# Attention output laid out by token block, and one ScalarE copy per PSUM bank for a batch of two steps

## The chip, the cores and the metric

The kernel runs on one core of one Trainium2 chip. The metric is the device time of one execution in microseconds; the median of 3 runs before the change is 198.72 us (198.62 to 199.81). The engines are named as in the profile: PE is TensorE's matmul side and PEld its weight load, DVE is VectorE, ACT is ScalarE, POOL is GpSimd, SP is SyncE, which starts most of the DMAs.

## What is computed

A linear attention with decay runs over 4 batches, 8 heads and 768 tokens with heads of 64, and its result goes through a two-layer network with a tanh gelu:

```python
for b in range(nb):                       # blocks of 64 tokens
    intra = einsum('bhic,bhjc->bhij', qb, kb) * Dmask
    intra = einsum('bhij,bhjd->bhid', intra, vb)
    inter = einsum('bhid,bhde->bhie', qb * lam_pow, kv_state)
    out[:, :, sl] = intra + inter
    kv_state = lam_block * kv_state + einsum('bhsd,bhse->bhde', kb * rev_pow, vb)
x = out.transpose(0, 2, 1, 3).reshape(3072, 512)
h = x @ w_in                              # 512 x 2048
g = 0.5 * h * (1 + tanh(c * (h + 0.044715 * h**3)))
return g @ w_out                          # 2048 x 512
```

## The kernel before

**Steps.** The attention is worked in 24 steps. A step is one block of 256 tokens of one batch and one half of the heads (4 of 8, as two pairs): step s is block s // 2 and half s % 2. Twelve blocks in all, three to a batch. Inside a step the kernel works with two chunks of 128 tokens. For each step there are: the casts of q (VectorE), k (ScalarE) and v (GpSimd) to fp16; the transposes of q and k, by TensorE for the steps up to 7 and by DMA from step 8 on (`FIRST_DMA_T`); the scores (L350); their mask on VectorE (`causal`, L360); the products with v, and the products with the carried state u, both into the same PSUM bank, one bank for each chunk; the products of k and v for the new state; the state's update on VectorE (L534) and its fp16 copy u on GpSimd (L542 or L549). Last `x_out` copies the two banks into the fp16 tile xT, which the network reads. Steps either go one at a time (`R`, which calls `scores` and `products`) or, from step 12 on, in `burst`, which takes two steps together: the banks O0 and O1 then hold both steps' 256 columns side by side. The bursts of two steps evacuate 13/14, 16/17, 18/19, 20/21 and 22/23; step 15 goes alone in `R` and step 12 alone in a burst.

**NARROW.** For the steps 13, 14, 16, 17, 20 and 21 the product with u is made by four matmuls of 64 rows and not two of 128, and in bank 1 the two heads of a pair stand with their partition halves exchanged. For these `x_out` copies bank 1 by two copies of 64 partitions (L509), each into the other half; the full copies are L513.

**Groups.** Blocks are gathered in seven groups, [0,1], [2], [3], [4,5], [6,7], [8,9] and [10,11]. Once a group's attention is finished, `queue_group` puts its network work, as small pieces, at the end of a list; `fill(n)` issues the next n pieces. First-layer pieces (L597, L874) make 512 columns in one bank, which a gelu on ScalarE (L601) copies out. Groups 1 to 6 make the second layer with sums of blocks (L646) and seven products (L676) in place of eight; groups 5 and 6 do so for the first layer too (`seven`, L775, with sums of x on VectorE at L754). Where a group has two blocks and the plain first layer, one matmul reads both blocks: two runs of 256 columns of xT.

**Order.** The order of the instructions on each engine is written out by hand (`pin` keeps it); an engine works its own list in order and waits at semaphores that the framework places from the tiles read and written. PSUM has eight banks, taken in turn by all tiles. The part that the change touches stands thus for steps 13 and 14: `burst((15, 16), (13, 14))` issues scores of 15 and 16, products of 13 and 14 (L446), the state products (L461), a wait, the u products (L474), the masks on VectorE, then the copies of both steps on ScalarE; `fill` follows with first-layer pieces, whose gelus queue behind those copies.

Of the kernel before, what the change touches and what calls it, by code (L numbers as in the profile page):

```python
# [9 lines left out]
FP16 = mybir.dt.float16  # L10
# [5 lines left out]
def kernel(  # L16
# [10 lines left out]
    nc = tc.nc  # L27
    pin = tc.keep_in_program_order
    P = 128
    B, H, S, D = q.shape  # L30
    SB = 256
# [19 lines left out]
    xtp = ctx.enter_context(tc.tile_pool(name="xtp", bufs=3))  # L51
# [287 lines left out]
    def half64(i):  # L339
        return slice(64 * i, 64 * i + 64)  # L340
# [21 lines left out]
                mask[:].unsqueeze(1).to_broadcast([P, 2, 2 * P]), ALU.mult))  # L362
        PTs[n] = t

    def products(n, s, banks=None, evacuate=True):


        OK, opened = banks or ([ps_M.tile([P, 512], FP32, tag="M", name=f"OK{c}")
                                for c in range(2)], set())

        def start(c, hl):
            if (c, hl) in opened:
                return False
            opened.add((c, hl))
            return True

        if n is not None:
            _, tk, tv = a16[n]
            last = (n // 2) % NSB == NSB - 1
            for jk in range(2):  # L380
                for hp in range(2):
                    for c, hl in TILES:
                        if c == 1 and last:
                            continue
                        pin(nc.tensor.matmul(
                            OK[c][half64(hl), 256 + hp * D : 256 + hp * D + D],
                            tk[half64(c), jk, 2 * hp + hl, :], tv[half64(c), jk, 2 * hp + hl, :],
                            start=start(c, hl), stop=(jk == 1), skip_group_check=True))
            Kps[n] = [t[:, 256:384] for t in OK]
        if s is None:  # L390
            return OK, opened
        sbg, half = divmod(s, 2)
        o = qkT.pop(s)
        PT = PTs.pop(s)
        _, _, tv = a16.pop(s)
        for hp in range(2):
            for jk in range(2):
                for c, hl in TILES:
                    pin(nc.tensor.matmul(  # L399
                        OK[c][half64(hl), hp * P : hp * P + P], tv[half64(c), jk, 2 * hp + hl, :],  # L400
                        PT[half64(c), hl, hp, jk, :], start=start(c, hl), stop=False,
                        skip_group_check=True))
        for c in range(2):
            if c == 0 and sbg % NSB == 0:
                continue
            u = us.pop((s, 0) if c else (s - 2, 1))
            for hp in range(2):
                pin(nc.tensor.matmul(OK[c][:, hp * P : hp * P + P], u[:, hp].rearrange("p l d -> p (l d)"),  # L408
                                     o[:, 0, :, hp, half64(c)], start=False, stop=True,
                                     skip_group_check=True))  # L410
        if evacuate:
            x_out(s, OK)
        return OK, opened

    def behind(ins):
# [7 lines left out]
    def burst(ns, ss, *mix, ahead=None):  # L423


        narrow = bool(NARROW & set(ss))
        for i, n in enumerate(ns):
            scores(n)
            if ahead and i == 0:
                ahead()  # L430
        O = [ps_M.tile([P, 2, 2, P], FP32, tag="M", name=f"O{c}") for c in range(2)]
        seen = set()

        def start(kind, c, hl):
            new = (kind, c, hl) not in seen
            seen.add((kind, c, hl))
            return new

        qTs = [qkT.pop(s) for s in ss]
        for i, s in enumerate(ss):  # L440
            PT, tv = PTs.pop(s), a16.pop(s)[2]
            for hp in range(2):
                for jk in range(2):
                    for c, hl in TILES:
                        to = hl ^ narrow * c
                        mm = nc.tensor.matmul(  # L446
                            O[c][half64(to), i, hp, :], tv[half64(c), jk, 2 * hp + hl, :],
                            PT[half64(c), hl, hp, jk, :], start=start("O", c, to), stop=False,
                            skip_group_check=True)
                        pin(mm)  # L450
        if ns:
            K = [ps_M.tile([P, 2, P], FP32, tag="M", name=f"K{c}") for c in range(2)]
        for i, n in enumerate(ns):
            _, tk, tv = a16[n]
            last = (n // 2) % NSB == NSB - 1
            for jk in range(2):
                for hp in range(2):
                    for c, hl in TILES:
                        if c == 1 and last:
                            continue  # L460
                        pin(nc.tensor.matmul(  # L461
                            K[c][half64(hl), i, hp * D : hp * D + D],
                            tk[half64(c), jk, 2 * hp + hl, :], tv[half64(c), jk, 2 * hp + hl, :],
                            start=start("K", c, hl), stop=(jk == 1), skip_group_check=True))
            Kps[n] = [t[:, i] for t in K]
        if narrow:
            behind(mm)
        for i, s in enumerate(ss) if narrow else ():
            u = [us.pop(key, None) for key in ((s - 2, 1), (s, 0))]
            for hp in range(2):  # L470
                for c, hl in TILES:
                    if u[c] is None:
                        continue
                    pin(nc.tensor.matmul(  # L474
                        O[c][half64(hl ^ c), i, hp, :], u[c][half64(hl), hp, :],
                        qTs[i][half64(hl), 0, :, hp, half64(c)], start=False, stop=True,
                        skip_group_check=True))
        for i, s in enumerate(ss) if not narrow else ():
            for c in range(2):
                if c == 0 and (s // 2) % NSB == 0:  # L480
                    continue
                u = us.pop((s, 0) if c else (s - 2, 1))
                for hp in range(2):
                    pin(nc.tensor.matmul(O[c][:, i, hp, :], u[:, hp].rearrange("p l d -> p (l d)"),
                                         qTs[i][:, 0, :, hp, half64(c)], start=False, stop=True,
                                         skip_group_check=True))
        for n in ns:
            causal(n)
        for i, s in enumerate(ss):
            x_out(s, [t[:, i].rearrange("p h t -> p (h t)") for t in O], swapped=narrow)  # L490
        sbg = ss[-1] // 2
        g, i = group_of[sbg]
        if ss[-1] % 2 == 1 and i == len(groups[g]) - 1:
            queue_group(g, *mix)
        for n in ns:
            update(n, 0)

    def x_out(s, OK, second=None, swapped=False):
        sbg, half = divmod(s, 2)
        g, i = group_of[sbg]  # L500
        if g not in xT:
            xT[g] = xtp.tile([P, 2, len(groups[g]), 2, SB], FP16, tag="xT", name=f"xT_{g}")
        dst = xT[g][:, half, i]
        for c in range(2):
            d = dst[:, :, c * P : (c + 1) * P].rearrange("p hp (t j) -> p hp j t", j=2)
            o = OK[c][:, 0:256].rearrange("p (hp j t) -> p hp j t", hp=2, j=2)
            if c == 1 and swapped:
                for hl in range(2):
                    pin(nc.scalar.activation(out=d[half64(hl)], in_=o[half64(1 - hl)], func=AF.Copy))  # L509
            elif c == 1 and second is not None:  # L510
                pin(second.tensor_copy(out=d, in_=o))
            else:
                pin(nc.scalar.activation(out=d, in_=o, func=AF.Copy))  # L513
# [66 lines left out]
    def queue_group(g, lead=0, per_set=0):  # L580
# [4 lines left out]

        def x(c):

            return xT[g][:, c // 2, :, c % 2, :]

        def by_block(t):  # L590
            return t.rearrange("p (b t) -> p b t", t=SB)
# [151 lines left out]
        def x_block(t, cs):  # L743
            if t in X_SUMS:
                return xsum[0][:, (t - 1) // 2, (t - 1) % 2, cs, :]
            C, T = t
            return xT[g][:, C, T, cs, :]

        def sum_x(m):
            if not xsum:  # L750
# [194 lines left out]

    def R(n, s, ahead=None, keep=False):

        if n is not None:
            scores(n)
        if ahead:  # L950
            ahead()
        products(n, s)
        if n is not None:
            causal(n)
        if s is not None and s % 2 == 1:
            g, i = group_of[s // 2]
            if i == len(groups[g]) - 1 and g > 0:
                queue_group(g)
        if n is not None and not keep:
            update(n, 0)  # L960
# [236 lines left out]
```

## Time and profile before

| | |
|---|---|
| median of 3 runs | 198.72 us (198.62 to 199.81) |
| the profiled execution | 198.66 us, of which the span is 196.9 us |
| PE busy | 191.0 us |
| ACT busy | 125.0 us |
| DVE busy | 145.9 us |
| POOL busy | 68.9 us |
| copies of 128x256 out of OK banks (one step) | 26, mean 452 ns, 9.9 us |
| copies of 128x256 out of O banks (bursts) | 16, mean 459 ns, 6.6 us |
| copies of 64x256 out of O banks (bursts, NARROW) | 12, mean 454 ns, 5.5 us |

The span goes from the first to the last instruction of the profiled execution, and its own time is some 1.8 us longer. A line of the profile's groups names the source line, the engine, the operation, the tile written and the tiles read, the count, the busy time and the mean duration; a line of the order of time gives the start, the duration, and in brackets how long the engine stood idle before it and what ended that. A line of the list of waits gives who waited for whom, the total in us, the number of times and the longest. The profile's slices are fortieths of the span, in tenths of busy time.

### The profile page before, as it was taken

The page shows a single profiled execution, that of the slowest core. Times are in us where ns is not written, and L with a number is a line of the kernel's source. Part 1 is how long each engine was busy: PE and PEld are TensorE (multiplying, and loading weights), DVE is VectorE, ACT ScalarE, POOL GpSimd, SP SyncE. Part 2 cuts the span into 40 slices and gives each one's busy share as a digit, 9 for nine tenths or more (in the row PEclk, how much of TensorE's full clock was granted, in tenths as well). Part 3 has the DMA queues.
Part 4 walks back from the last instruction along what each step waited for, and adds up shares of the span by engine and source line. Part 5 has one row for each costly group of instructions (what it writes and reads, how often), then busy time and mean ns, then how long its engine had stood idle before and what let it go on. Part 6 is the DMA issues. An engine that isn't in the chain of part 4 may idle for free.

```text
span 196.9 us, 5962 instructions
## 1 busy us (share of the span) xinstructions
PE 191.0 (97%) x2451; PEld 139.4 (71%) x2453; DVE 145.9 (74%) x291; ACT 125.0 (63%) x255; POOL 68.9 (35%) x85
## 2 busy tenths in 40 slices
PE   8979999999999999999999999999999999999993
PEld 2556544446888888654678854578888888888882
DVE  4797722889999889849989925999657987487620
ACT  3673878357874685676855379844867866679221
POOL 6594213456554841068623415056002030002000
PEclk9999999999999999999999999999999999999999
DMA  5999999999999999999996998710211300020205
GB/s 169 290 323 385 386 387 388 296 295 288 244 217 222 257 343 223 214 270 264 252 279 148 269 314 115 163 33 0 53 59 51 109 4 2 0 110 28 82 16 199
DMA packets 62811, 38.13 MB, mean 194 GB/s; under 512 B 18624, under 2 KB 55744, under 8 KB 62784
## 3 DMA queue, kind: packets, MB, share of 16 engines
q1 hardware_dynamic: 62240, 37.50, 76.6%
q8 instruction: 19, 0.31, 0.7%
q10 hardware_dynamic: 544, 0.26, 0.5%
q14 instruction: 8, 0.07, 0.1%
HBM read 27.26 MB, written 6.29 MB: 170 GB/s over the span
## 4 chain that ended last, share of the span: by engine, by line
PE 87%; SPq 4%; DMA 4%; ACT 3%; issue 1%
PE Hps L597 23%; PE MX L676 18%; PE MY L676 9%; PE HX L775 7%; PE O2ps L612 7%; PE MW L676 4%; DMA wi<-in_moe_w_in_dram 4%; SPq L70 4%; PE HY L775 4%; PE S L350 3%; PE Hps L874 3%; PE HW L775 2%; PE OK L408 2%; PE O L446 1%; PE OK L399 1%; PE Tps L321 1%
## 5 line engine op out<-in xcount | busy, mean ns | idle before, releaser
L597 PE MATMUL Hps<-xT,w_in 128*128 128x512 f16 (+1 forms) x288 | 50.5, 332 | 0.0
L597 PEld LDWEIGHTS <-w_in 128*128 128x128 f16 x288 | 27.8, 98 | 19.3
L601 ACT ACTIVATE gT<-Hps 128x512 f16<-128x512 f32 x56 | 32.4, 598 | 9.8 <-PE Hps L597 9.2
L360 DVE TENSOR_TENSOR PT<-S,mask 128x512 f16<-128x512 f32 x48 | 30.3, 682 | 8.3 <-PE S L350 8.3
L676 PEld LDWEIGHTS <-gs 128*128 128x128 f16 x320 | 31.2, 98 | 3.6
L266 POOL TENSOR_TENSOR v<-v,dv 128x512 f16<-128x512 f32 x24 | 27.0, 1128 | 18.5 <-PE Hps L597 9.6
L549 POOL TENSOR_TENSOR u<-t,lumask 128x256 f16<-128x256 f32 x29 | 21.4, 748 | 29.8 <-DVE t L534 20.5
L676 PEld LDWEIGHTS <-gT 128*128 128x128 f16 x240 | 23.1, 98 | 3.7 <-ACT gT L601 0.6
L676 PE MATMUL MX<-w_sum,gs 128*128 128x256 f16 x160 | 21.4, 273 | 0.0
L646 DVE TENSOR_TENSOR gs<-gT 128x1024 f16<-128x1024 f16 (+1 forms) x24 | 17.8, 750 | 3.3 <-ACT gT L601 3.3
L282 DVE TENSOR_TENSOR qk<-q,dq 128x512 f16<-128x512 f32 x23 | 18.1, 792 | 1.5 <-DMA q<-in_q_dram 1.3
L295 ACT ACTIVATE qk<-k 128x512 f16<-128x512 f32 x23 | 14.4, 626 | 7.4 <-DMA k<-in_k_dram 6.9
L728 POOL TENSOR_TENSOR o<-u,q 128x512 f32<-128x512 f32 (+1 forms) x5 | 5.9, 1184 | 36.9 <-ACT u L693 36.9
L612 PE MATMUL O2ps<-w_out,gT 128*128 128x512 f16 x64 | 14.6, 379 | 0.0
L513 ACT ACTIVATE xT<-OK 128x256 f16<-128x256 f32 x26 | 9.9, 452 | 6.5 <-PE OK L408 6.1
L775 PEld LDWEIGHTS <-ws 128*128 128x128 f16 x128 | 12.4, 98 | 1.7 <-DVE xs L754 0.2
L693 ACT ACTIVATE u<-MX 128x256 f32<-128x256 f32 x18 | 6.9, 384 | 7.3 <-PE MX L676 7.3
L612 PEld LDWEIGHTS <-gT 128*128 128x128 f16 x64 | 6.1, 98 | 6.6
L676 PE MATMUL MY<-w_out,gs 128*128 128x256 f16 x80 | 10.7, 273 | 0.0
L350 PEld LDWEIGHTS <-qkT 64*64 64x64 f16 x384 | 6.0, 106 | 6.6 <-issue 3.6
L542 POOL TENSOR_TENSOR u<-t,lamu 128x128 f16<-128x128 f32 x11 | 6.1, 559 | 12.8 <-DVE t L534 7.2
L789 DVE COPY u<-HX 128x512 f32<-128x512 f32 x8 | 5.5, 688 | 6.8 <-ACT gT L793 4.3
(102 smaller groups left out, 326.5 us busy)
## 6 DMA issues: line engine op xcount, KB each, us to landing
q<-in_q_dram SPq DMA_DIRECT2D x24, 256.0 KB, 4.8
k<-in_k_dram SPq DMA_DIRECT2D x24, 256.0 KB, 5.0
v<-in_v_dram SPq DMA_DIRECT2D x23, 256.0 KB, 5.3
out_dram<-o SPq DMA_DIRECT2D x23, 256.0 KB, 4.1
wo<-in_moe_w_out_dram SPq DMA_DIRECT2D x4, 1024.0 KB, 9.5
wi<-in_moe_w_in_dram SPq DMA_DIRECT2D x4, 512.0 KB, 8.1
wi<-in_moe_w_in_dram SPq DMA_DIRECT2D x2, 1024.0 KB, 12.7
v<-in_v_dram ACTq DMA_DIRECT2D x1, 256.0 KB, 4.2
```

What stands on the lines that cost most here:

```text
L266: pin(nc.gpsimd.tensor_tensor(wide(tv[:]), ld32[s][2][:], decay(dv, s), ALU.mult))
L282: pin(q_eng.tensor_tensor(wide(tq), q32[:], decay(dq, s), ALU.mult))
L295: pin(nc.scalar.activation(out=wide(tk), in_=k32[:], func=AF.Copy))
L350: pin(nc.tensor.matmul(Sps[hl][half64(c), hp, jk, :], o[half64(hl), 1, jk, hp, half64(c)], o[half64(hl), 0, :, hp, half64(c)], start=True, ...
L360: pin(nc.vector.tensor_tensor(t[:, hl].rearrange("p b c d -> p b (c d)"), Sps[:].rearrange("p b c d -> p b (c d)"), mask[:].unsqueeze(1).t ...
L549: pin(nc.gpsimd.tensor_tensor(u[:], state[half][:].unsqueeze(2).to_broadcast([P, 2, 2, D]), lumask[:, 2 * half : 2 * half + 2, :].unsqueez ...
L597: pin(nc.tensor.matmul(by_block(Hps[:, i, :]), w_in16[:, c, f * P : (f + 1) * P], x(c), start=(c == 0), stop=(c == NC - 1)))
L601: pin(nc.scalar.activation(out=dst, in_=Hps[:], func=AF.Gelu_apprx_tanh))
L612: pin(nc.tensor.matmul(O2[tau][0][:], gT[:, f % HF, f // HF, tau * P : (tau + 1) * P], w_out16[:, f, :], start=(n == 0), stop=(n == NF - 1)))
L646: pin(nc.vector.tensor_tensor(g_rows(m, i), g_rows(a, i), g_rows(b, i), op))
L676: pin(nc.tensor.matmul(dst, lhsT, rhs, start=(opens and i == 0), stop=(closes and i == HF - 1), skip_group_check=True))
L775: pin(nc.tensor.matmul(dst[:, i, :], w_in_block(a, slice(c, c + 1), slice(f * P, f * P + P))[:, 0], x_block(b, slice(c, c + 1))[:, 0], sta ...
```

## The change

xT held, for each group, the axes half, block, pair, token; it now holds block, half, pair, token. Steps that follow one another (half 1 of one block and half 0 of the next among them) thus stand side by side. `x_out` takes a list of steps and one slice of each bank that covers all of them, and makes one copy for each bank (or, in bank 1 of NARROW steps, two of 64 partitions) for the whole list. `burst` calls it once. The readers of xT take the new axes. `products` and `R` also get a branch for steps in NARROW.

```diff
@@ products
-            x_out(s, OK)
+            x_out((s,), [t[:, 0:256] for t in OK], swapped=s in NARROW)
@@ burst
-        for i, s in enumerate(ss):
-            x_out(s, [t[:, i].rearrange("p h t -> p (h t)") for t in O], swapped=narrow)
+        x_out(ss, [t[:, 0 : len(ss)].rearrange("p i h t -> p (i h t)") for t in O], swapped=narrow)
@@ x_out
-    def x_out(s, OK, second=None, swapped=False):
-        sbg, half = divmod(s, 2)
+    def x_out(ss, O, second=None, swapped=False):
+
+        sbg, half = divmod(ss[0], 2)
         g, i = group_of[sbg]
         if g not in xT:
-            xT[g] = xtp.tile([P, 2, len(groups[g]), 2, SB], FP16, tag="xT", name=f"xT_{g}")
-        dst = xT[g][:, half, i]
+            xT[g] = xtp.tile([P, len(groups[g]), 2, 2, SB], FP16, tag="xT", name=f"xT_{g}")
+        r = 4 * i + 2 * half
+        dst = xT[g].rearrange("p b a h t -> p (b a h) t")[:, r : r + 2 * len(ss)]
         for c in range(2):
-            d = dst[:, :, c * P : (c + 1) * P].rearrange("p hp (t j) -> p hp j t", j=2)
-            o = OK[c][:, 0:256].rearrange("p (hp j t) -> p hp j t", hp=2, j=2)
+            d = dst[:, :, c * P : (c + 1) * P].rearrange("p r (t j) -> p r j t", j=2)
+            o = O[c].rearrange("p (r j t) -> p r j t", j=2, t=D)
@@ queue_group
-            return xT[g][:, c // 2, :, c % 2, :]
+            return xT[g][:, :, c // 2, c % 2, :]
...
-            return xT[g][:, C, T, cs, :]
+            return xT[g][:, T, C, cs, :]
@@ products, for s in NARROW (before: none)
+        if s in NARROW:
+            between()
+            behind(mm)
+            u = [us.pop(key, None) for key in ((s - 2, 1), (s, 0))]
+            for hp in range(2):
+                for c, hl in TILES:
...
@@ R
+        def first():
+            if n is not None:
+                scores(n)
+            if ahead:
+                ahead()
+
+        if s in NARROW:
+            products(n, s, between=first)
+        else:
+            first()
+            products(n, s)
```

More of the change, by code (lines that the diff above doesn't have):

```diff
@@ L363, in causal, with products @@
         PTs[n] = t
-    def products(n, s, banks=None, evacuate=True):
+    def products(n, s, banks=None, evacuate=True, between=None):
         OK, opened = banks or ([ps_M.tile([P, 512], FP32, tag="M", name=f"OK{c}")
@@ L398, in products @@
                 for c, hl in TILES:
+                    to = hl ^ (c if s in NARROW else 0)
+                    mm = nc.tensor.matmul(
+                        OK[c][half64(to), hp * P : hp * P + P], tv[half64(c), jk, 2 * hp + hl, :],
+                        PT[half64(c), hl, hp, jk, :], start=start(c, to), stop=False,
+                        skip_group_check=True)
+                    pin(mm)
+        if s in NARROW:
[4 more added lines that the diff above has]
+                for c, hl in TILES:
+                    if u[c] is None:
+                        continue
                     pin(nc.tensor.matmul(
-                        OK[c][half64(hl), hp * P : hp * P + P], tv[half64(c), jk, 2 * hp + hl, :],
-                        PT[half64(c), hl, hp, jk, :], start=start(c, hl), stop=False,
+                        OK[c][half64(hl ^ c), hp * P : hp * P + P], u[c][half64(hl), hp, :],
+                        o[half64(hl), 0, :, hp, half64(c)], start=False, stop=True,
                         skip_group_check=True))
-        for c in range(2):
+        for c in range(2) if s not in NARROW else ():
             if c == 0 and sbg % NSB == 0:
@@ L946, in R @@
     def R(n, s, ahead=None, keep=False):
[L948 to L952, printed above, removed]
+        def first():
[8 more added lines that the diff above has]
+            products(n, s)
         if n is not None:
```

## The prediction

> **What bounds the kernel now.** I read the page's busy shares and slices first, then the chain of waits, the list of who waited for whom, and last the order of time around each of the five places where a batch of two steps leaves its banks.
>
> ```profile
> span 196.9 us, 5962 instructions
> ...
> PE 191.0 (97%) x2451; PEld 139.4 (71%) x2453; DVE 145.9 (74%) x291; ACT 125.0 (63%) x255; POOL 68.9 (35%) x85
> ...
> PE   8979999999999999999999999999999999999993
> ...
> PEclk9999999999999999999999999999999999999999
> ```
>
> TensorE is busy in every slice but the first and the last, at its full clock. The 5.9 us in which it is not busy (196.9 - 191.0) lie almost wholly in two places: 20.00 - 17.55 = 2.45 us in the first 20 us, and 6.90 - 3.61 = 3.29 us after 190 us, in the final copy and store (both from the table of busy time by stretch). Neither holds a batch of two steps. So ScalarE's 63% says nothing by itself: the change pays only where TensorE waits for ScalarE.
>
> The chain of waits, asked for 94 to 101 us, seems to show a large prize. 26.0 + 12.9 = 38.9% of these 7 us lie on the copies to be merged:
>
> ```profile
> 94.92 0.35 PE O L474 x12
> 95.28 0.45 ACT xT L513
> ...
> 95.73 0.46 ACT xT L509
> ...
> 96.20 0.45 ACT xT L509
> ...
> 96.67 0.46 ACT xT L513
> ...
> 98.08 0.79 ACT gT L601 x2
> ...
> 99.05 0.61 ACT gT L601
> ...
> 99.71 1.16 PE MX L676 x9
> ```
>
> A chain only says what released what. It doesn't say that TensorE stood still meanwhile. The order of time on TensorE and the list of waits say what was really lost:
>
> ```profile
> 95.18 3.63 PE L597 MATMUL Hps<-xT,w_in 128*128 128x512 f16 x16
> 98.65 2.22 PE L676 MATMUL MX<-w_out,gT 128*128 128x256 f16 x16
> ```
>
> ```profile
> PEld L676 <- ACT gT L601: 0.4, 1, 0.4
> ```
>
> TensorE worked through 16 matmuls of the first layer from 95.18 us and began the second layer's first product at 98.65. Seven of that product's eight matmuls were issued; the eighth needs the gelu that ended at 99.66 and started at 99.712, while its predecessor had started at 99.303. A matmul of 256 columns takes 0.109 us from start to start here (0.87 us for eight in the whole chain), so **the loss is 99.712 - 99.303 - 0.109 = 0.30 us**. I took the start-to-start distance of all neighbouring TensorE matmuls in the same way: after 20 us this is the only gap above 0.2 us. The others are 0.10 to 0.16 us each, nearly all where matmuls of 64 and of 128 rows change over, and hang on no copy that the change touches.
>
> **What the Trainium skill says.** "ScalarE: Activation LUTs", section "What ACT_TABLE_LOAD costs", prices an ACTIVATE without pointer operands at 186 ns + 0.833 ns per column and says that back-to-back ones overlap by about 93 ns. The trace agrees for plain copies: 384 ns at 256 columns against 399, 598 ns at 512 against 612. The xT copies, with their interleaved fp16 output, show 455 ns at 256 columns, some 70 more. "PSUM — Partial Sum Buffer", section "PSUM bank collisions raise a hardware error", has two engines kept off one bank and quadrant even at different columns. The trace fits: in the batch of steps 13 and 14 the first copy, whose own columns were done with the O matmuls at about 94.7 us, started only at 95.27, after the last L474. It was waiting on the bank, so a copy of the whole bank has nothing more to wait for.
>
> **The change part by part.**
>
> *Layout of xT.* Step s writes 512 consecutive columns before and after. The sums on VectorE read 512 consecutive columns before and after. The first layer's two-block matmuls read two runs of 256 columns, now 1024 columns apart and not 512. Their present spacing is 6.91 us / 32 = 0.216 us, the same as the second layer's 7.77 / 36 = 0.216 with one unbroken run, so a break in the run costs nothing at today's distance. I take 0 for the wider distance; the other end stands with the rivals.
>
> *Fewer copies.* Five batches have two steps. The three in the NARROW set (13/14, 16/17, 20/21) go from 2 full and 4 half-partition copies to 1 and 2; the two others (18/19, 22/23) from 4 to 2. In all 26 copies become 13. One copy of 512 columns isn't in the trace. From below: 598 ns, the gelu of 512 columns out of a bank. From above: 455 + 256 x 0.833 = 668 ns, with the skill's slope, which the trace's own (598 - 384) / 256 = 0.836 repeats. I take 0.65. In the NARROW batches the copies stand end to end, 0.47 us from start to start (six from 95.27 to the next gelu at 98.08 = 2.81 us); three of 0.65 + 0.01 make 1.98 us, so 0.83 us is saved each. Range: 3 x 0.61 to 3 x 0.68, saving 0.77 to 0.98. In the unshifted batches the copies overlap, 0.29 to 0.33 us apart; the last batch's four end after 161.59 - 160.21 = 1.38 us, and two of 512 columns, about 0.50 apart, end after 0.50 + 0.65 = 1.15 us: 0.23 us saved. Sum: 3 x 0.83 + 2 x 0.23 = 3.0 us of ScalarE.
>
> *Where it lands on the path.* At 95.27 only. The last four gelus there start at 98.08, 98.58, 99.05 and 99.53, back to back behind the copies. With copies that end near 97.25, the third gelu is limited by its own matmuls: 12 of the 16 end at about 95.18 + 12 x 0.218 = 97.80, and in the steady stretch before, a gelu starts 0.2 us after its piece; so it runs from 98.0 to 98.6 us, 0.8 us before TensorE wants it at 99.41. **The whole 0.30 us goes**, and would go for any copy up to (2.81 - 0.30) / 3 = 0.83 us. What is late next there is nothing: the second product of that phase wants the fourth gelu only after 100.4 us.
>
> *The other four batches* give 0. At 118.28 and 155.61 ScalarE falls behind as much, but TensorE goes on with the first layer and with the second products, and no TensorE wait shows there; at 126.29 the sums start at 129.15, 1.2 us after the copies end. The last batch could lose. There the first sum wants step 22 from both banks, 160.98 before, about 161.36 after, or 160.21 + 2 x 0.668 = 161.55 without overlap. VectorE comes to that sum at 161.46 in any case, so the cost is 0 (taken) to 0.1 us, and the matmuls HY wait for this sum already (0.17 us on the weight loads).
>
> *The new branch for NARROW steps in the single-step products.* The steps that pass through it are 0 to 11 and 15, and none is in the set, so its extra wait and changed order are never emitted: 0.
>
> *Does the 0.30 us stay?* TensorE runs 0.3 us earlier from 99.7 on. What could be late by then is a transpose by DMA: those for step 21 land at 123.98 us against use at 125.15, and wait on TensorE itself for their buffer; step 19's land at 113.7 against 116.6. Covered, with over 1 us.
>
> Sum, against the profiled execution's own 198.66 us (span 196.87 and 1.8 around it): 198.66 - 0.30 = 198.36. That execution lies 0.06 below the median of the three runs shown, so 198.4 on their scale.
>
> **The rivals.**
> *No gain.* The freed ScalarE time is taken back, by a 512-column copy above 0.83 us or because the awaited gelu is then held by something that the chain hides. For it: only one place pays, and by 0.15% of the time. Against: the six gelus from 89.38 to 93.69 us, with no copies ahead of them, each found ScalarE idle for 0.27 to 0.40 us first. Time: 198.7, or 198.8 with the last batch's 0.1.
> *Slower, by the reads of xT.* Two-block matmuls of 512 columns are 160 in L597 and 16 in L874. If two runs 2048 bytes apart stream worse than runs 1024 bytes apart, each pays; TensorE has no slack, so all of it shows. Above 0.30 / 176 = 1.7 ns each the change is slower than before; at 10 ns it is 198.36 + 1.76 = 200.1. Against: today's break in the run costs nothing measurable, 0.216 us with it and without.
> *More than forecast.* Also the 0.17 us at HY and some of the mode changes vanish: 198.2. Against: the former hangs on VectorE's queue.
>
> **How the numbers follow.** Forecast 0.64 (198.2 to 198.6), no gain 0.25 (198.6 to 199.0), slower by the reads 0.06 (mostly 199 to 201), more than forecast 0.05. Two of the three runs shown are 0.1 us apart and the third is 1.1 higher, so I give 0.2 us for the median's own scatter: the range is 198.0 to 199.0, which leaves out the slower rival. About 1%, 2 us, is what a measurement of this kernel can tell from no change, and neither main case reaches it; slower by more needs over 13 ns per two-block matmul: 0.04. Faster by more has no cover in the profile, since TensorE's waits for ScalarE after 20 us don't add up to 1 us: 0.02.
>
> **What would show it.** 13 xT copies out of O banks with 512 columns at 0.60 to 0.67 us, and none in place of the 26; ScalarE busy about 122 to 124 us in place of 125.0, less than the copies' sum where overlaps vanish. In the stretch after steps 13/14 the gelus follow their matmuls, and the weight loads' wait of 0.4 us for gT is gone. First-layer matmuls of 512 columns still 379 ns and 0.216 us apart. The prediction is wrong if that wait stays, if the matmuls' spacing grows, or if a new wait of TensorE appears at the last batch, near 161.9 us, or at a burst.

## The result and the profile after

The changed kernel takes 198.44 us (median of 18 runs, 198.29 to 199.01) against 198.75 us before (18 runs beside them): ratio 0.9982, 95% interval 0.9974 to 0.9989. The forecast was 198.4 us, and that no more than one TensorE stall of 0.30 us would go. The profiled execution took 198.45 us with a span of 196.7 us, so 1.79 us lie outside the span, as before.

The edit moves the lines behind it: L474, L484, L597, L676 and L754 of the kernel before are L488, L498, L612, L691 and L769 now. The page of the changed kernel, its head, the busy times and TensorE's slices:

```profile
span 196.7 us, 5947 instructions
...
PE 190.0 (97%) x2451; PEld 139.2 (71%) x2453; DVE 147.1 (75%) x291; ACT 123.7 (63%) x242; POOL 70.3 (36%) x85
...
PE   8869999999999999999999999999999999999993
```

ScalarE has 13 instructions fewer (242 against 255) but is busy only 1.3 us less. The 13 merged copies show why. The groups of ScalarE, with the shapes kept apart (busy us, mean ns of one | idle before):

```profile
L528 ACT ACTIVATE xT<-O 128x512 f16<-128x512 f32 x7 | 4.9, 744 | 4.3 <-PE O L488 2.2 <-PE O L498 1.6 <-PE O L460 0.4
...
L524 ACT ACTIVATE xT<-O 64x512 f16<-64x512 f32 x6 | 4.5, 742 | 0.1
...
L528 ACT ACTIVATE xT<-O 128x256 f16<-128x256 f32 x2 | 0.9, 458 | 0.3 <-PE O L460 0.2
```

A merged copy takes 744 ns, above the 668 ns that the prediction had as its upper end. Before, the copies out of O banks came to 6.6 + 5.5 = 12.1 us, of which two for step 12 (0.9 us) stay as they were; the other 26 with 11.2 us became 13 with 4.9 + 4.5 = 9.4 us. ScalarE's busy time falls by less than this 1.8 us, since the copies that went had partly overlapped each other.

The stretch behind steps 13/14, first the chain of waits for 94 to 101 us:

```profile
94.93 0.33 PE O L488 x12
95.26 3.56 PE Hps L612 x16
98.82 1.75 PE MX L691 x16
```

The detour through ScalarE is gone from the chain; it stays on TensorE. In the order of time of the same stretch (start, us, engine, line), TensorE's product is no longer broken after its seventh matmul, and the gelus begin at 97.56 and not at 98.08:

```profile
98.66 1.91 PE L691 MATMUL MX<-w_out,gT 128*128 128x256 f16 x16
```

```profile
95.28 0.74 ACT L528 ACTIVATE xT<-O 128x512 f16<-128x512 f32 x1 [0.46 <-PE O L488]
96.05 1.49 ACT L524 ACTIVATE xT<-O 64x512 f16<-64x512 f32 x2
97.56 2.07 ACT L616 ACTIVATE gT<-Hps 128x512 f16<-128x512 f32 x4
```

Sixteen matmuls took 2.22 us before and 1.91 us now. That is 0.31 us, the whole difference of the medians. But it isn't all that happened. I matched every TensorE matmul of one trace with the same matmul of the other and subtracted their starts. From 20 us on the difference moves at only four places: by -0.31 us at 99.7 us, by -0.09 us in two small steps at 126.7 and 137.7 us, and by +0.15 us at 161.9 us. They sum to -0.25 us; the 0.06 us between that and the medians' -0.31 is within the medians' scatter. The last of the four is a loss. There the matmuls HX read x itself, and the matmuls HY behind them wait for the first sum of parts of x after the last batch, steps 22/23. Before, in the order of time around 161 us:

```profile
161.46 0.41 DVE L754 TENSOR_TENSOR xs<-xT 128x512 f16<-128x512 f16 x1
161.92 0.33 PEld L775 LDWEIGHTS <-ws 128*128 128x128 f16 x4 [0.17 <-DVE xs L754]
```

and after:

```profile
159.82 1.34 ACT L528 ACTIVATE xT<-O 128x512 f16<-128x512 f32 x2 [1.65 <-PE O L498]
...
161.20 0.43 DVE L769 TENSOR_TENSOR xs<-xT 128x512 f16<-128x512 f16 x1
...
161.68 0.33 PEld L790 LDWEIGHTS <-ws 128*128 128x128 f16 x4 [0.31 <-DVE xs L769]
```

TensorE is 0.39 us earlier here than before, but the sum is only 0.26 us earlier. It needs step 22 from both banks, and the second merged copy ends at 159.82 + 1.34 = 161.16 us, just ahead of the sum. VectorE's own instruction before the sum ends at 161.15 us, but that doesn't hold it: in the kernel before, the sum started at 161.458 us while the instruction ahead of it ended only at 161.535.

### The profile page after: what moved, and what is told of

Same layout as the page of the kernel before. It is cut to its first block, busy times and chain, and to the rows that moved or that the text cites. A ratio compares the mean times of both kernels' runs of the same rounds, so it can differ in the third digit from the quotient of the medians.

```text
span 196.7 us, 5947 instructions
## 1 busy us (share of the span) xinstructions
PE 190.0 (97%) x2451; PEld 139.2 (71%) x2453; DVE 147.1 (75%) x291; ACT 123.7 (63%) x242; POOL 70.3 (36%) x85
## 4 chain that ended last, share of the span: by engine, by line
PE 89%; SPq 4%; DMA 4%; ACT 0%; issue 0%
PE Hps L612 25%; PE MX L691 18%; PE MY L691 9%; PE HX L790 7%; PE O2ps L627 7%; PE MW L691 4%; DMA wi<-in_moe_w_in_dram 4%; SPq L70 4%; PE HY L790 4%; PE S L350 3%; PE Hps L889 3%; PE HW L790 2%; PE OK L422 2%; PE O L460 1%; PE OK L400 1%; PE Tps L321 1%
## 5 line engine op out<-in xcount | busy, mean ns | idle before, releaser
L612 PE MATMUL Hps<-xT,w_in 128*128 128x512 f16 (+1 forms) x288 | 50.5, 332 | 0.0
L612 PEld LDWEIGHTS <-w_in 128*128 128x128 f16 x288 | 27.8, 98 | 19.3
L266 POOL TENSOR_TENSOR v<-v,dv 128x512 f16<-128x512 f32 x24 | 28.0, 1169 | 16.9 <-DMA v<-in_v_dram 16.0
L691 PEld LDWEIGHTS <-gs 128*128 128x128 f16 x320 | 31.2, 98 | 3.6
L691 PEld LDWEIGHTS <-gT 128*128 128x128 f16 x240 | 23.2, 98 | 3.3 <-ACT gT L616 0.2
L691 PE MATMUL MX<-w_sum,gs 128*128 128x256 f16 x160 | 21.4, 273 | 0.0
L661 DVE TENSOR_TENSOR gs<-gT 128x1024 f16<-128x1024 f16 (+1 forms) x24 | 16.5, 696 | 2.3 <-ACT gT L616 2.3
L691 PE MATMUL MY<-w_out,gs 128*128 128x256 f16 x80 | 10.7, 273 | 0.0
L804 DVE COPY u<-HX 128x512 f32<-128x512 f32 x8 | 5.5, 689 | 6.8 <-ACT gT L808 4.4
```

The lines of the kernel that those rows point to most:

```text
L266: pin(nc.gpsimd.tensor_tensor(wide(tv[:]), ld32[s][2][:], decay(dv, s), ALU.mult))
L612: pin(nc.tensor.matmul(by_block(Hps[:, i, :]), w_in16[:, c, f * P : (f + 1) * P], x(c), start=(c == 0), stop=(c == NC - 1)))
L661: pin(nc.vector.tensor_tensor(g_rows(m, i), g_rows(a, i), g_rows(b, i), op))
L691: pin(nc.tensor.matmul(dst, lhsT, rhs, start=(opens and i == 0), stop=(closes and i == HF - 1), skip_group_check=True))
```

## The experiments

In all of them the time of the kernel before is that of runs on the same chip beside them, 198.74 to 198.79 us. Besides the median I give TensorE's shift: how much earlier (-) or later (+) its matmuls start than in the kernel before, counted from each trace's own shift at 70 us, where no batch has yet been touched.

| kernel | median us (before) | at 110 us | 110 to 150 us | 160 to 170 us | end |
|---|---|---|---|---|---|
| the change | 198.44 (198.75) | -0.31 | -0.09 | +0.15 | -0.25 |
| e8_after_again | 198.46 (198.74) | -0.31 | -0.09 | +0.15 | -0.26 |
| e1_layout_only | 198.74 (198.76) | 0.00 | 0.00 | 0.00 | 0.00 |
| e2_only_13_14 | 198.44 (198.76) | -0.31 | 0.00 | 0.00 | -0.31 |
| e8_e2_again | 198.41 (198.74) | -0.31 | 0.00 | 0.00 | -0.31 |
| e3_all_but_13_14 | 199.00 (198.76) | 0.00 | -0.09 | +0.14 | +0.05 |
| e8_e3_again | 198.83 (198.74) | 0.00 | -0.09 | +0.15 | +0.06 |
| e4_all_but_22_23 | 198.56 (198.76) | -0.31 | -0.09 | 0.00 | -0.40 |
| e4_again | 198.53 (198.75) | -0.31 | -0.09 | 0.00 | -0.40 |
| e9_e4_third | 198.52 (198.79) | -0.31 | -0.09 | +0.01 | -0.39 |
| e5_unbroken_output | 198.41 (198.75) | -0.31 | -0.09 | 0.00 | -0.40 |
| e6_lead4 | 198.66 (198.75) | -0.31 | -0.09 | -0.05 | -0.03 |
| e7_one_copy_twice | 199.22 (198.75) | +0.06 | -0.09 | +0.15 | +0.12 |

(For e6_lead4 the column for 160 to 170 us leaves out the piece of 0.44 us that this kernel moves ahead. At 180.7 us it loses 0.44 us against the kernel before.)

### Which batch carries the gain: e1 to e4

All four undo the merging for some batches and keep the new layout; only the condition differs:

```diff
-        x_out(ss, [t[:, 0 : len(ss)].rearrange("p i h t -> p (i h t)") for t in O], swapped=narrow)
+        if CONDITION:   # False | ss[0] == 13 | ss[0] != 13 | ss[0] != 22
+            x_out(ss, [t[:, 0 : len(ss)].rearrange("p i h t -> p (i h t)") for t in O], swapped=narrow)
+        else:
+            for i, s in enumerate(ss):
+                x_out((s,), [t[:, i].rearrange("p h t -> p (h t)") for t in O], swapped=narrow)
```

> The new layout of xT, but each step of a batch still leaves by its own copies (26 copies of 256 columns). Theory (the gain is one TensorE stall of 0.30 us behind the copies of steps 13/14): no change from the kernel before, 198.75 us within 0.1, the stall of 0.30 us near 99.3 us is back, and the start-to-start distance of 512-column first-layer matmuls stays 0.216 us. Rival (the layout itself does it, or costs something that the copies pay back): a change of 0.2 us or more either way without any copy merged.

> Only the batch of steps 13/14 is merged. Theory: 0.3 us faster than before, and a little faster than the whole change, 198.3 us, since the last batch isn't merged and the wait of the matmuls HY near 161.9 us doesn't grow (0.05 us lost there as before, not 0.20). Rival (ScalarE's freed time helps at all five batches alike): a fifth to a quarter of the gain, 198.65 us.

> The four other batches are merged, 13/14 is not. Theory: the 0.30 us stall stays and the last batch's wait grows by 0.15 us, so 0.1 to 0.15 us slower than before, 198.85 us. Rival (the gain is spread over the batches): three quarters of the gain stay, 198.5 us.

> All batches merged but the last, 22/23. Theory: the stall of 0.30 us is gone and the loss of 0.15 us at the last batch too: 198.3 us, 0.15 us faster than the whole change, and HY starts within 0.06 us of its place behind HX. Rival (the 0.2 us lost there has another cause, such as VectorE's queue): the gap of 0.20 us between HX and HY stays, 198.45 us.

The layout alone changes nothing: ratio 0.9998 (0.9992 to 1.0005), and the stall is back. This is the wait in e1_layout_only between 94 and 101 us:

```profile
PEld L695 <- ACT gT L620: 0.4, 1, 0.4
```

Only 13/14 merged brings the whole measured gain: 198.44 us, ratio 0.9985 (0.9973 to 0.9997). All others merged without 13/14 bring none: 199.00 us, ratio 1.0007 (0.9998 to 1.0015), and the same wait of 0.4 us stands in its trace. So the gain is one stall's, and the rival that ScalarE's freed time helps at all batches alike falls. The table's columns add up across the kernels: -0.31 goes with 13/14 alone, +0.15 with 22/23 (it is there in e3 and gone in e2 and e4), -0.09 with 16/17 and 18/19 together; nothing moves behind 20/21, which leaves its banks at 155 us. The 198.3 us expected of e2 left out that e2 also lacks those 0.09 us: its trace is 0.06 us ahead of the whole change, which the medians don't tell apart.

Those -0.09 us were not expected. The larger part is at 137.7 us, where before a product HX started 0.17 us behind its predecessor and now 0.11: it overwrites a bank that VectorE first copies out, and that copy (L789 before, L804 after) started at 136.94 us and now at 136.41, 0.53 us earlier while TensorE there was only 0.33 earlier. The traces show where VectorE got ahead: behind 16/17, where its first sum gs waits for gelus that queue behind the copies. Before, then after:

```profile
122.72 0.69 DVE L646 TENSOR_TENSOR gs<-gT 128x1024 f16<-128x1024 f16 x1 [2.00 <-ACT gT L601]
```

```profile
121.88 0.76 DVE L661 TENSOR_TENSOR gs<-gT 128x1024 f16<-128x1024 f16 x1 [1.45 <-ACT gT L616]
```

The sum starts 0.85 us earlier where TensorE is only 0.30 us earlier, and VectorE keeps the lead up to the copy at 136.41 us. No kernel with 16/17 alone merged was run, and the smaller step at 126.7 us has no cause found.

The median of e4 misses its expectation. In its trace the last batch's loss is gone and TensorE is 0.40 us ahead, yet three loads gave 198.56, 198.53 and 198.52 us, no better than the whole change. More below.

### What a copy of 512 columns costs: e5

```diff
-            d = dst[:, :, c * P : (c + 1) * P].rearrange("p r (t j) -> p r j t", j=2)
+            d = dst[:, :, c * P : (c + 1) * P].rearrange("p r (j t) -> p r j t", j=2)
```

> The whole change, but every copy into xT writes its columns in the order in which they stand in the bank (pieces of 64 adjacent fp16 values) and not every second place; the interleaving of the tokens of a chunk is left out, so the output rows stand in another order. It measures why a merged copy took 744 ns where 598 to 668 were forecast. Theory (the output's step of two places costs each column about 0.28 ns): copies of 512 columns at about 600 ns and of 256 at about 385, the wait at HY near 161.9 us back to 0.05 us, 198.3 us. Rival (512 columns read across two steps of one bank cost it, whatever the output): 744 ns stay.

Its groups of copies into xT:

```profile
L528 ACT ACTIVATE xT<-OK 128x256 f16<-128x256 f32 x26 | 8.5, 381 | 6.5 <-PE OK L422 6.2 <-PE OK L400 0.3
L528 ACT ACTIVATE xT<-O 128x512 f16<-128x512 f32 x7 | 4.1, 597 | 4.7 <-PE O L488 2.2 <-PE O L498 2.1 <-PE O L460 0.4
```

With unbroken output a copy takes 381 ns for 256 columns and 597 for 512, as the other ScalarE copies do. So writing every second fp16 place costs 452 - 381 = 71 ns on 256 columns and 744 - 597 = 147 ns on 512: 0.28 to 0.29 ns for each column. The rival falls too, since 512 columns read across two steps take 597 ns. The prediction had read the 71 ns as fixed and added only 0.833 ns per further column. With the shorter copies the loss at 161.9 us is gone too (0.00 in the table), though the median, 198.41 us, is only 0.03 below the change's.

### How much cover there is: e7

```diff
         x_out(ss, [t[:, 0 : len(ss)].rearrange("p i h t -> p (i h t)") for t in O], swapped=narrow)
+        if ss[0] == 13:
+            x_out(ss, [t[:, 0 : len(ss)].rearrange("p i h t -> p (i h t)") for t in O], only=0)
```

(`only=0` restricts `x_out` to bank 0; the lines in `x_out` that do so are left out here.)

> The whole change, and in the batch of steps 13/14 the merged copy of bank 0 is made twice, the same values again, 0.75 us more of ScalarE ahead of the gelus. Theory (the stall is what ScalarE's work there exceeds the cover by; with the change the awaited gelu ended 0.24 us before it was needed): 0.75 - 0.24 = 0.5 us of stall near 99.5 us, 198.95 us, slower than the kernel before. Rival (TensorE's 0.30 us came from elsewhere, the changed layout or the number of copies): 198.45 us, unchanged.

199.22 us, ratio 1.0029 (1.0019 to 1.0039): slower than before. Order of time on ScalarE, then on TensorE:

```profile
97.64 0.75 ACT L530 ACTIVATE xT<-O 128x512 f16<-128x512 f32 x1
98.24 2.05 ACT L618 ACTIVATE gT<-Hps 128x512 f16<-128x512 f32 x4
```

```profile
98.73 0.93 PE L693 MATMUL MX<-w_out,gT 128*128 128x256 f16 x7
99.86 1.16 PE L693 MATMUL MX<-w_out,gT 128*128 128x256 f16 x9 [0.20 <-ACT gT L618]
```

The stall returns behind the seventh matmul: 99.861 - 99.389 - 0.109 = 0.36 us, not 0.5, because the repeated copy overlaps the gelu behind it and delays it by 98.24 - 97.64 = 0.60 us. In the changed kernel the awaited gelu ends at 99.14 us and TensorE starts the matmul that needs it at 99.42; less the 0.05 us that lie between the two where TensorE does wait, this leaves 0.23 us of cover, and 0.60 - 0.23 = 0.37, within 0.01 us of the stall. The mechanism thus holds in both directions, with the sizes that the trace gives. The median is higher than this stall explains; the repeats below take that up.

### Can the loss at the last batch be had back: e6

```diff
-    burst((), (22, 23), 3, 4)
+    burst((), (22, 23), 4, 4)
```

> The whole change, and behind the last batch one piece more of the earlier group's second layer goes ahead of the first-layer products of the last group (4 in place of 3). Theory (HY waits 0.20 us for the first sum of x, which the longer merged copies hold up): the sum has 0.44 us more, the gap between HX and HY goes, 0.15 to 0.2 us faster than the whole change, 198.25 us. Rival (the order of the pieces behind it is finely set): the gain is lost at a later wait, 198.45 us or more.

198.66 us. The wait at HY went, but the rival was right: the piece moved ahead is missing later. Order of time near 180 us:

```profile
179.98 0.69 DVE L812 TENSOR_TENSOR q<-HX,q 128x512 f32<-128x512 f32 x1
...
180.73 0.60 PE L790 MATMUL HX<-xs,w_in 128*128 128x256 f16 x4 [0.35 <-DVE q L812]
```

HX is written into a bank that VectorE has to read first, and nothing stood in between any more: 180.728 - 180.110 - 0.109 = 0.51 us lost there, against 0.07 in the change.

### What the medians add to the traces: the repeats

> The kernel with all batches merged but 22/23, loaded and timed once more, since its median of 198.56 us stood 0.25 us above what its trace's gains add up to (0.41 us from 43 us on, with 0.2 us lost before 43 us, where no batch is touched). If the start's scatter is by load and not by kernel: 198.3 to 198.4 us this time. If the merged batches 16/17 to 20/21 cost something that the trace hides: 198.55 us again.

> The changed kernel once more, to see whether the part of the time outside the span (1.79 us before and after, 1.81 and 2.04 in two loads of the kernel with all but 22/23 merged, 2.03 and 2.10 in two others) belongs to a kernel or to a load. By kernel: 1.79 us outside the span and 198.44 us again. By load: either value, and the median moves by 0.2 us with it.

> Only 13/14 merged, once more. From the traces' gains (0.30 us, and neither the 0.06 us near 137.7 us nor the loss of 0.15 us near 161.9 us): 198.44 us again, with the stall near 99.3 us gone and HY within 0.06 us of its place. By load: up to 198.65 us with 2.04 us outside the span.

> All but 13/14 merged, once more. The trace's stages add up to 0.09 us slower than before (stall kept, 0.06 us won near 137.7, 0.15 us lost near 161.9 us): 198.85 us, if the 0.24 us more outside the span belonged to that load; 199.0 us again, if it belongs to the kernel.

> All batches merged but 22/23, a third load. Its trace says 0.42 us faster than before, its medians of 198.56 and 198.53 us say 0.2 us. If the missing 0.2 us is by load, as it was for the kernel with all but 13/14 merged (199.00, then 198.83 us): 198.35 us with 1.79 us outside the span and nothing lost before 43 us. If it belongs to this kernel: 198.55 us once more.

The change and e2 repeat within 0.03 us (198.46 and 198.41 us). The kernel without 13/14 gave 199.00 us, then 198.83, which agrees with the traces' +0.06 us. The kernel without 22/23 did not come down in three loads.

Load (one time that the program is put on a chip) or kernel? The span was noted for every run, to 0.1 us, and not only for the profiled one. That gives the time outside the span:

| kernel | runs | us outside the span |
|---|---|---|
| before, beside the experiments | 195 | 1.73 to 1.86 |
| the change, both loads | 33 | 1.73 to 1.85, mean 1.79 |
| e1, e2, e5, e6 | 96 | 1.73 to 1.86 |
| e3, two loads | 13 and 13 | up to 2.09 (mean 1.97), then up to 1.97 (mean 1.87) |
| e4, three loads | 19, 21 and 21 | up to 2.10, 2.08 and 2.09; means 1.96, 1.96 and 1.93 |
| e7 | 22 | 2.06 to 2.17, mean 2.11 |

Chance in a load doesn't explain this: e4 has the longer time in all three of its loads, and 195 runs of the kernel before, on the same chips, never have it. The time outside the span goes with the kernel as it was built, and in e3 it also varied from load to load: 0.10 of the 0.17 us between its two medians lie there. It holds some 0.15 us of e4's median. In e7 it is 0.3 us of the 0.47 us by which the median stands above the kernel before, where the trace says 0.12. e4's median span is 196.6 us in each load, against 196.65 and 196.7 us for the change, so that at most 0.1 us of the 0.15 us which its trace wins shows in the spans. Why these three kernels take longer outside the span is not known. So the +0.15 us at the last batch is shown in TensorE's order of time, but that undoing it gains device time is not.

No kernel tried is measurably better than the change.

## Why the prediction was right, and where its steps were off

*The stall.* The working named one place, one wait and 0.30 us. The traces show -0.31 us there. Without this merge the stall stays (e1, e3), with this merge alone it goes (e2), and with more ScalarE work at this place it comes back (e7). So this place holds the gain. The reading that a copy of the whole bank has nothing more to wait for held as well: the first copy started at 95.28 us, against 95.27 before. The trace shows that it waits for TensorE (0.46 us, for L488); whether the hardware rule that the prediction names is the reason, no run tests.

*The price of a merged copy.* Mis-sized: 0.65 us taken, 0.598 to 0.668 as the range, 0.744 measured. The failed term is "455 + 256 x 0.833": the interleaved output costs each column, not each instruction. For 13/14 three copies took 97.56 - 95.28 = 2.28 us and not 1.98, so 0.53 us (2.82 - 2.28, before rounding) were saved there and not 0.83. The conclusion stood because the limit of 0.83 us for a copy, worked out beside it, was not reached (2.28 / 3 = 0.76).

*The cover.* "0.8 us before TensorE wants it" became 0.28 us (99.42 - 99.14). The third gelu started at 98.53 us and not at 98.0: 0.3 us of that is the copies' later end (97.54 us, not 97.25), and the rest is that the first two gelus still stand ahead of it in ScalarE's queue, which the working left out.

*ScalarE in sum.* 3.0 us forecast. By the starts it was 0.53 us at 13/14 and 0.54 each at 16/17 and 20/21; at the last batch 1.38 us became 1.34, not 1.15, since two merged copies follow each other in 0.61 us and not 0.50. Busy time fell by 1.3 us.

*The last batch.* Taken at 0, with 0.1 us as the other end; it was 0.15 us of TensorE's time, outside the range. The term that failed is the end of the two merged copies, set at about 161.36 us: on the clock of before it is 160.21 + 1.34 = 161.55 us, which the working had as its worst case, and VectorE came to the sum at 161.46 as it said. That TensorE and VectorE are 0.39 us ahead here plays no part, for the copies start as much earlier. In e3, whose TensorE starts HX at about the old time, the sum also starts 0.15 us behind HX (161.20 - 161.05 in the change), and the loss is the same 0.14 us:

```profile
161.42 0.60 PE L794 MATMUL HX<-xT,w_in 128*128 128x256 f16 x4
161.57 0.42 DVE L773 TENSOR_TENSOR xs<-xT 128x512 f16<-128x512 f16 x1
```

The prediction had named a new wait of TensorE near 161.9 us as a sign that it is wrong. A wait of 0.05 us there grew to 0.20 us, so that part of it, "the other four batches give 0", was wrong.

*The other three batches.* Taken at 0; 16/17 and 18/19 gave 0.09 us, most of it by VectorE's way. That the forecast of -0.30 and the medians' -0.31 agree so closely is in part luck: -0.09 and +0.15 were both left out, and they nearly cancel. The 1% that the prediction takes a measurement to tell apart was too coarse: the interval is 0.08% to either side, and the gain of 0.18% stands clear of it.

*Wider reads.* The matmuls of 512 columns take the same 379 ns (before, the same line stood with L597 and the same numbers):

```profile
L612 PE MATMUL Hps<-xT,w_in 128*128 128x512 f16 x160 | 35.7, 379 | 0.0
```

Their starts stay 0.216 us apart in the changed kernel and in e1. With e1 at 0.00 in every column the rival that ended slower is refuted. Nothing shows of the new branch for NARROW steps either: the steps that go through `R` are 0 to 11 and 15, none of them in NARROW, and both traces hold 2451 matmuls.

## What to carry to other kernels

Look for a stall on the engine that bounds, in its own starts, before pricing what a chain of waits runs through: here 39% of a 7 us stretch lay on the copies and 0.30 us was to be had. Merging two transfers saves their fixed part but makes the first half arrive as late as the second, so ask who needs the first half. For changes of a few tenths of a microsecond, matching each instruction's start in two traces separates gains and losses that the medians blur; and compare the time outside the span over all runs before a median is laid to the edit.

## What the runs showed of the hardware that was not expected

A ScalarE copy from PSUM to fp16 costs 0.28 to 0.29 ns more per column when it writes every second place (452 against 381 ns at 256 columns, 744 against 597 at 512). Copies of 64 partitions into the other partition half don't overlap their neighbours: 0.47 us from start to start at 455 ns, 0.75 at 742 ns, where full copies of 455 ns follow each other in 0.29 to 0.33 us and those of 744 in 0.61. No run separates the 64 partitions from the change of half. The time outside the span is not the same for all kernels: 1.73 to 1.86 us in every run of the kernel before, the change, e1, e2, e5 and e6, but 2.06 to 2.17 us in every run of e7 and up to 2.10 us in each load of e4. That difference is as large as the whole gain of this change.
